# Attention in tiles of 128 tokens of one row, and the first expert's weights brought in one part in three tiles

## The chip, the cores and the metric

The kernel runs on one core of a Trainium2 chip. The metric is the time that the device takes for one launch, in microseconds (us): before, the median of three runs was 1137.16 us (1136.15 to 1142.16). The chip's engines are named as in the profile: PE is the matrix engine (TensorE) and PEld its weight loads, DVE the VectorE, ACT the ScalarE, POOL the GpSimd, SP the SyncE, which here only issues transfers; a name with a q behind it (SPq) is an engine's queue of transfers.

## The reference, cut to what matters

```python
def _attn_ref(q, k, v):                 # each 8 rows x 8 heads x 576 tokens x 64
    scores = scale * np.matmul(q, k.transpose(0, 1, 3, 2))
    gamma = 1.0 - 2.0 ** (-5.0 - np.arange(H, dtype=np.float32))
    rel = pos[:, None] - pos[None, :]
    Dmat = np.where(rel >= 0, gamma[:, None, None] ** rel[None, :, :], 0.0)
    return np.matmul(scores * Dmat[None, :, :, :], v)

def reference(...):
    attn_out = _attn_ref(q, k, v)
    x = attn_out.transpose(0, 2, 1, 3).reshape(B * S, H * D)   # 4608 tokens x 512
    x = _moe_ref(x, w_gate, w1, w2)          # 8 experts; every token goes to its best one
    return _moe2_ref(x, w_gate, w1, w2)      # 8 experts; each takes 576 tokens
```

The attention has no softmax: it is causal, with a decay of gamma to the power of the distance. So it can be computed a piece of a row at a time, with a state of 64x64 per head that is carried from piece to piece: outputs of a piece = (its queries times the state before it) + (masked scores inside the piece, times its values).

## The kernel before, in words

The program runs setup, then `attention`, then the two expert layers. Attention gives 36 tiles of 128 tokens x 512 channels (the rows of X), computes the gate's logits of the first expert layer for each, and stores the tiles to memory (`Xs`). The expert layers start when attention is over; the first expert's rows are gathered and turned while attention still runs its last tiles.

A tile before is 64 tokens of each of two batch rows: `pr, j = divmod(t, 9)`, row pair `pr` and position `j` of nine. Tokens of the one row lie in partitions 0 to 63, those of the other in 64 to 127. `wk` and `ld` are pools of buffers in on-chip memory, `ps` one of accumulators.

Attention's stages are listed in `stages`, each with an offset: in step `s` of the loop at the end of `attention`, stage `f` with offset `off` works on tile `s - off`. Every instruction of that loop keeps its written place on its engine. One step does, in this order on PE:

- `scores`: the products of keys and queries (`pS<-qT,kT`), the queries times the state (`pO<-st,qT`, left out for j = 0), the update of the state (`pS<-vf,k`, left out for j = 8). Each is 16 matmuls of 64x64x64 in fp32, four at a time in the four quadrants of the array (`ZW`). DVE then masks the scores (`s`) and adds the update to the state (`st`).
- `xlow`, of the tile two steps ago: one f16 matmul that leaves the low part of the turned output (`less`), then eight small f16 matmuls for the logits (`tp<-wg1s,xTh`). ACT makes the low part `xTl`.
- `kturn`, of the tile two steps ahead: four transposes of k (`tp<-ct,k`), copied out by ACT.
- `logits`: four small matmuls with `xTl`.
- `outputs`: 16 matmuls of masked scores and values (`pO<-vf,s`, `pO<-vs,s`); DVE then writes the rows `xr`. The values `vf` are scaled on POOL, which also copies half of them to the other partitions (`vs`).
- `xturn` of the tile one step ago, `qturn` of the tile two steps ahead: four transposes each.
- `route`, once for a group of up to four tiles (`starts`): the choice of the expert and its weight, on DVE, ACT and POOL.

`load` brings k, q and v of the tile six steps ahead, as two transfers each (a half of the partitions each), issued by SP in the same written order, in which `store` also stands.

`early` is a generator of which the loop takes one part per step from step `AFTER` = 24 on. Its first part issues the first three pieces of the first expert's first weights (`stage<-in_moe_w_dram`, 512 KB each); from two steps later on, each of four parts casts a piece to f16 (`w1h` on ACT, the low part on DVE or POOL); then come the lists and the gather of the 384 rows that the first expert takes from the first 27 tiles, and their normalising and turning.

In the profile all instructions of the loop have the line L102, that of the helper which keeps the order, so tiles are told apart by their names.

Of the kernel before, what the change touches and what calls it, by code (L numbers as in the profile page):

```python
# [21 lines left out]
BIG = 1048576.0  # L22
TA = 27
SA = 3
AFTER = 24
LEAD_IN = 6
T0 = (76, 88)
LATE = 3
SOON = 3
# [14 lines left out]
def consts_np():  # L44
    import numpy as np
    p=np.arange(128)
    g=1.0-2.0**(-5.0-np.arange(8))
    cols=[]
    for j in range(9): cols.append(g[None,:]**(63-p%64-64*j)[:,None])
    for j in range(9): cols.append(g[None,:]**(p%64-63.0+64*j)[:,None]*2.0**-3)  # L50
    tok=np.zeros((128,36))
    for t in range(36):
        pr,j=divmod(t,9)
        tok[:,t]=(2*pr+p//64)*576+64*j+p%64
    cols.append(tok)
    cols.append(np.eye(128))
    j=p[:,None]; i=p[None,:]
    cols.append((i[:,:64]>=j%64)*1.0)
# [5 lines left out]
CO=dict(gk=(0,72),go=(72,144),tok=(144,180),id=(180,308),m=(308,372),lt=(372,500),p=(500,501),blk=(501,509),sel=(509,525))  # L64

class K: pass

# [48 lines left out]
def attention(k, q, kk_, v, wg1, X, after):  # L116
    tc = k.tc
    nc = InOrder(tc, k.nc)
# [9 lines left out]
    D = [K() for _ in range(NT)]  # L128
    for t, d in enumerate(D):
        d.t = t  # L130
        d.pr, d.j = divmod(t, 9)
# [8 lines left out]
    half = lambda n: slice(64 * n, 64 * n + 64)  # L140
    at = lambda n, d: k.c(n)[:, 8 * d.j:8 * d.j + 8]
    zh = lambda x: x.rearrange("p (h z) d -> p z h d", z=2)

    def load(d):
# [15 lines left out]
    ZW = ((0, 0), (1, 1), (0, 1), (1, 0))  # L160

    def across(pt, x, more=False):

# [13 lines left out]
    def qturn(d):  # L177
        d.qT = turned(d, d.iq, "qT")

    state = [None]  # L180
    pend = []

    def scores(d):
# [3 lines left out]
        pS = ps.tile([128, 2, 512], F32, name="pS")  # L187
        s = pS[:, :, 0:256].rearrange("p z (h i) -> p z h i", i=64)
        n = pS[:, :, 256:512].rearrange("p w (h e) -> p w h e", e=64)
# [3 lines left out]
        for hp in range(4 if d.j else 0):  # L193
            for z, w in ZW:
                mm(d.o[half(w), z, hp, :], d.qT[half(z), hp, half(w)], state[0][half(z), w, hp, :], start=hp == 0, stop=False)
        if d.j < 8:
            for hp in range(4):
                for w, z in ZW:
                    h = 2 * hp + z
                    mm(n[half(z), w, hp, :], d.ik[half(w), h, :], d.vf[half(w), h, :], start=True, stop=True)  # L200
        d.s = wk.tile([128, 2, 4, 64], F32, name="s", bufs=2)
        nc.vector.tensor_tensor(d.s, s, k.c('m')[:, None, None, :].to_broadcast([128, 2, 4, 64]), op=OP.mult)
        if d.j < 8:
            t = wk.tile([128, 2, 4, 64], F32, name="st", bufs=3)
            if d.j:
                nc.vector.tensor_tensor(t, n, state[0], op=OP.add)
            else:
                nc.vector.tensor_copy(t, n)
            state[0] = t

    def outputs(d):
        for hp in range(4):
            for z, w in ((0, 0), (0, 1), (1, 0), (1, 1)):
                r = w ^ z
                mm(d.o[half(w), z, hp, :], d.s[half(r), z, hp, :], d.vs[half(r), hp, :] if z else d.vf[half(r), 2 * hp, :],
                   start=hp == 0 and d.j == 0, stop=hp == 3)
        p = P[d.g]
        if d.gj == 0:
            p.lgs = wk.tile([128, 9, 8], F32, name="lgs")
# [11 lines left out]
    def xlow(d):  # L231
        d.xl = wk.tile([128, 4, 128], F16, name="xTl", bufs=3)
        f = lambda x: x.rearrange("p c i -> p (c i)")
        mm(f(d.pt), k.less8, f(d.xh), start=False, stop=True)
        nc.scalar.activation(d.xl, d.pt, AF.Copy, scale=256.0)
        d.lg = ps.tile([128, 8], F32, name="tp", bufs=4)
        for c in range(4):
            for n in range(2):
                mm(d.lg, d.xh[:, c, :], wg1[:, c, 8 * n:8 * n + 8], start=c + n == 0, stop=False)

    def logits(d):
        for c in range(4):
            mm(d.lg, d.xl[:, c, :], wg1[:, c, 0:8], start=False, stop=c == 3)
        nc.scalar.activation(P[d.g].lgs[:, d.gj, :], d.lg, AF.Copy)

    def route(d):
        p = P[d.g]
        if d.gj < p.n - 1:
            return
        N = p.n  # L250
        T = slice(p.t0, p.t0 + N)
        L = p.lgs[:, :N, :]
# [12 lines left out]
        es = wk.tile([128, 9], F32, name="es")[:, :N]  # L265
        nc.vector.tensor_reduce(es, ex, op=OP.add, axis=AX.X)
        nc.vector.tensor_scalar(es, es, 1e-9, None, op0=OP.add)
        gt = wk.tile([128, 9], F32, name="gt")[:, :N]
        nc.vector.reciprocal(gt, es)
        nc.gpsimd.tensor_copy(p.xrows[:, :N, 513], k.c('tok')[:, T])  # L270
        nc.gpsimd.tensor_copy(p.xrows[:, :N, 512], gt)
        pend.append(p)
# [15 lines left out]
    store()  # L288
    for _ in after:
        pass  # L290
    k.nc = nc.nc
    ctx.close()

# [32 lines left out]
    k.wn = k.xn = 0  # L326


def load_half(k, o, w, n, dve=0, spare=False, steps=True, behind=False):


    tc, nc = k.tc, k.nc
# [23 lines left out]
    stages = []  # L356
    for i in range(3):
        load(i)
    for i in range(4):
        yield  # L360
        t = stages[i]
# [275 lines left out]
    nc.vector.tensor_copy(k.cnt, pb[:, 1, :])  # L637


def early(k, X, w1):  # L640


    nc = k.nc
    first = load_half(k, k.w[0], w1, 1, 2)
    next(first)
    yield
    yield
    for _ in range(4):
        next(first, None)
        yield  # L650
# [936 lines left out]
def program(tc, q, kk, v, wg1, w11, w12, wg2, w21, w22, consts, out, dbg=None):  # L1587
# [10 lines left out]
    k.wgl = split_gate(k, wg2, "wg2")  # L1598
    select_setup(k)
    k.w = {0: K()}  # L1600
    attention(k, q, kk, v, g1, X, early(k, X, w11[0]))
    open_ffn(k)
    rest = moe1(k, X, X1, w11, w12)
    k.pin = False
# [35 lines left out]
```

## Time and profile before

| | us |
|---|---|
| median of three runs | 1137.16 (1136.15 to 1142.16) |
| the profiled execution, its own time | 1137.33 |
| its span in the trace | 1135.3 |
| PE busy over the span | 1034.0 |
| DVE busy | 595.7 |
| ACT busy | 433.9 |
| POOL busy | 295.8 |

The span is what the trace covers; 2.0 us of the execution lie outside it. Busy times are sums over the whole span, so they don't say which engine sets the pace in attention, which is the first fifth of it: there, the rows by stage and by wait further down have to be read. A duration in the trace runs from an instruction's start to its end; matmuls overlap, so what a group of them takes on PE is the distance between the starts of two groups.

### The profile page before, as it was taken

How to read it: one execution, taken by the hardware profiler on the slowest of the kernel's cores; microseconds unless marked ns; L12 is line 12 of the kernel's file. 1: busy time of each engine (PE TensorE's matmuls, PEld its weight loads, DVE VectorE, ACT ScalarE, POOL GpSimd, SP SyncE). 2: the span in 40 equal slices, each digit the busy share in tenths (PEclk: the TensorE clock that was granted, in tenths of full speed). 3: DMA queues.
4: the chain of work that ended last, by engine and by line, in shares of the span. 5: the costliest groups of instructions: out<-in, count | busy, mean ns of one | idle time of the engine just before them, and what ended most of it. 6: DMA issues, size and time to landing. Idle time of an engine off the chain costs nothing. (4 is left out here: it accounts for less than half of the span.)

```text
span 1135.3 us, 28053 instructions
## 1 busy us (share of the span) xinstructions
PE 1034.0 (91%) x11515; PEld 666.8 (59%) x11515; DVE 595.7 (52%) x1589; ACT 433.9 (38%) x747; POOL 295.8 (26%) x569
## 2 busy tenths in 40 slices
PE   5888958688999999999979989998999999899996
PEld 4777746555656564747447534655465756567572
DVE  2334425568566665648553366847565656634140
ACT  2444434447354554546442133423232333234240
POOL 4342333313213021212140022333133141341101
PEclk9998988979999999999989999999999999999998
DMA  7787889449777777878786033377475673774221
GB/s 167 160 212 183 191 223 217 135 130 256 187 158 195 163 195 171 179 178 209 204 172 110 11 108 124 122 182 162 113 172 119 160 176 104 199 200 139 85 71 43
DMA packets 308663, 178.41 MB, mean 157 GB/s; under 512 B 242544, under 2 KB 275312, under 8 KB 308528
## 3 DMA queue, kind: packets, MB, share of 16 engines
q1 hardware_dynamic: 298064, 144.20, 53.2%
q0 software_dynamic: 10464, 32.34, 9.1%
q8 instruction: 93, 1.52, 0.6%
q14 instruction: 42, 0.34, 0.1%
HBM read 116.78 MB, written 31.28 MB: 130 GB/s over the span
## 5 line engine op out<-in xcount | busy, mean ns | idle before, releaser
L487 PE MATMUL ph<-xT,w1h 128*128 128x320 f16 (+4 forms) x2048 | 367.4, 296 | 6.3 <-DVE hl L493 3.2
L487 PEld LDWEIGHTS <-w1h 128*128 128x128 f16 x2048 | 197.3, 99 | 77.4 <-issue 13.1
L487 PE MATMUL ph<-xT,w1l 128*128 128x320 f16 (+4 forms) x1024 | 230.9, 296 | 0.0
L513 PE MATMUL py<-w2h,hh 128*128 128x512 f16 x536 | 204.1, 381 | 2.2 <-DVE key L1268 2.2
L513 PE MATMUL py<-w2h,hl 128*128 128x512 f16 x536 | 203.9, 380 | 0.0
L513 PE MATMUL py<-w2l,hh 128*128 128x512 f16 x536 | 203.9, 380 | 0.0
L513 PEld LDWEIGHTS <-hh 128*128 128x128 f16 x1072 | 103.2, 98 | 119.0 <-issue 3.6
L492 ACT ACTIVATE hh<-ph 128x576 f16<-128x576 f32 (+4 forms) x136 | 83.5, 614 | 194.1 <-PE ph L487 189.9
L493 DVE SCALAR_TENSOR_TENSOR hl<-ph,hh 128x576 f16<-128x576 f32 (+4 forms) x136 | 97.2, 715 | 76.8 <-ACT hh L492 75.6
L487 PEld LDWEIGHTS <-w1l 128*128 128x128 f16 x1024 | 99.9, 99 | 32.7 <-issue 0.7
L373 DVE SCALAR_TENSOR_TENSOR w1l<-stage,w1h 128x1024 f16<-128x1024 f32 x60 | 73.1, 1223 | 60.1 <-ACT w1h L370 59.4
L513 PEld LDWEIGHTS <-hl 128*128 128x128 f16 x536 | 52.5, 98 | 60.4 <-issue 0.8
L373 DVE SCALAR_TENSOR_TENSOR w2l<-stage,w2h 128x1024 f16<-128x1024 f32 x64 | 78.1, 1222 | 6.0 <-ACT w2h L370 4.6
L418 ACT ACTIVATE x1r<-py 128x512 bf16<-128x512 f32 x40 | 23.9, 597 | 119.2 <-PE py L513 78.9
L370 ACT ACTIVATE w2h<-stage 128x1024 f16<-128x1024 f32 x64 | 66.9, 1047 | 0.0
L370 ACT ACTIVATE w1h<-stage 128x1024 f16<-128x1024 f32 x60 | 62.2, 1047 | 4.4 <-DMA stage<-in_moe_w_dram 4.4
L404 POOL DMA_INDIRECT xg<-X1s,ix x40 | 45.6, 1139 | 50.8 <-DVE zf L1372 31.2
L102 DVE TENSOR_TENSOR s<-pS,ct 128x512 f32<-128x512 f32 x36 | 24.8, 688 | 64.4 <-PE pS L102 64.4
L102 POOL TENSOR_TENSOR vf<-v,ct 128x512 f32<-128x512 f32 x36 | 37.5, 1042 | 74.8 <-DMA v<-in_v_dram 64.0
L1446 POOL DMA_INDIRECT out_dram<-x1r,ti x20 | 22.2, 1110 | 130.0 <-ACT x1r L1445 106.8
L571 POOL COPY x1r<-sc 128x1 f32<-128x1 f32 x37 | 12.1, 328 | 156.1 <-DMA X1s<-x1r 84.5
L1446 POOL DMA_INDIRECT out_dram<-w2T,ti x20 | 21.4, 1071 | 109.8 <-ACT w2T L1445 85.3
(358 smaller groups left out, 1479.3 us busy)
## 6 DMA issues: line engine op xcount, KB each, us to landing
stage<-in_moe_w_dram SPq DMA_DIRECT2D x128, 512.0 KB, 4.4
k<-in_k_dram SPq DMA_DIRECT2D x72, 128.0 KB, 4.1
q<-in_q_dram SPq DMA_DIRECT2D x72, 128.0 KB, 4.3
v<-in_v_dram SPq DMA_DIRECT2D x72, 128.0 KB, 4.0
X1s<-x1r SPq DMA_DIRECT2D x33, 257.0 KB, 3.7
Xs<-xr SPq DMA_DIRECT2D x6, 1028.0 KB, 6.2
Xs<-xr SPq DMA_DIRECT2D x3, 771.0 KB, 6.1
xg<-X1s,ix POOLq DMA_INDIRECT x40, 4.3
```

The source lines that it names most:

```text
L102: return lambda *args, **kw: self.tc.keep_in_program_order(f(*args, **kw))
L370: d = nc.scalar.activation(at(h, i), t, AF.Copy, scale=128.0)
L373: d = nc.vector.scalar_tensor_tensor(at(l, i), t, 128.0, at(h, i), op0=OP.mult, op1=OP.subtract)
L404: nc.gpsimd.indirect_dma_start(out=xg[:M], out_offset=None, in_=src, in_offset=bass.IndirectOffsetOnAxis(ap=gidx[:M], axis=0))
L418: d = nc.scalar.activation(q.bitcast(mybir.dt.bfloat16), x, AF.Square, accum_out=sc[:, 0:1])
L487: pe(k, nc.tensor.matmul(ph[:, z, :b], x[:, c, F], xT[:, y + c, a:a + b], start=i == 0, stop=i == 11))
L492: nc.scalar.activation(oh, src, AF.Relu)
L493: nc.vector.scalar_tensor_tensor(ol, src, 0.0, oh, op0=OP.max, op1=OP.subtract)
L513: pe(k, nc.tensor.matmul(py, x[:, f, S], y[:, f, :], start=i == 0, stop=i == 23))
L571: nc.gpsimd.tensor_copy(xr[:, 513:514], sc[:, 5:6])
L1446: nc.gpsimd.indirect_dma_start(out=out2 if tail else out, out_offset=bass.IndirectOffsetOnAxis(ap=ti, axis=0), in_=y, in_offset=None)
```

## The change

A tile becomes 128 tokens of one row. Of a row's 576 tokens four such tiles are made, which leaves 64; the leftovers of two rows make a tile as before (`tail`). In a row pair the tiles alternate between the two rows: n = 0 to 7 is piece n//2 of row n%2, n = 8 the tail. So there are 32 tiles of 128 tokens of one row (eight of them the first of their row) and 4 tails. The same 128 x 36 tokens are in the 27 tiles and in the 9 after them, in another order. The state is kept per row.

On PE a tile that is not a tail now has: `begun` 8 matmuls of 64 columns for the queries times the state, each with 64 of the array's rows; `scores` 8 of 128 columns, each with 64 rows, then the state's update as 8 of 64 columns, now in a `tp` buffer; `outputs` 8 of 64 columns that use the whole array. All of it stays fp32. The logits' first matmuls are 4 of 16 columns in place of 8 of 8 columns, and stand in `logits`; `kturn` stands behind it. On DVE the masked scores are 128x1024 in place of 128x512, the state's update 128x256 in place of 128x512, and `route` has one more addition. The copies `vs` on POOL are gone. `load` issues one transfer of 128 partitions for each of k, q and v.

The first expert's weights leave `early`: they get a generator of their own, which takes a part at step 4 and then at every third step (`CAST`), with the first three pieces' loads in three parts (`spread`) and all low parts on POOL. What is left of `early` starts at step 30, where it stood before.

```diff
-AFTER = 24
+CAST = (4, 3)
+EARLY = (30, 1)
...
     def load(d):
         for src, name in ((kk_, "k"), (q, "q"), (v, "v")):
             t = ld.tile([128, 8, 64], F32, name=name, bufs=dict(k=7, q=5, v=5)[name])
-            for w in range(2):
-                nc.sync.dma_start(t[half(w)], src[2 * d.pr + w, :, half(d.j), :].rearrange("h p d -> p h d"))
+            if d.tail:
+                for w in range(2):
+                    nc.sync.dma_start(t[half(w)], src[d.b + w, :, 512:576, :].rearrange("h p d -> p h d"))
+            else:
+                nc.sync.dma_start(t, src[d.b, :, 128 * d.j:128 * d.j + 128, :].rearrange("h p d -> p h d"))
...
-        d.vs = wk.tile([128, 4, 64], F32, name="vs", bufs=3)
-        for w in range(2):
-            nc.gpsimd.tensor_copy(d.vs[half(1 - w)], zh(d.vf)[half(w), 1])
...
+    def begun(d):
+
         d.pO = ps.tile([128, 2, 512], F32, name="pO")
         d.o = d.pO[:, :, 0:256].rearrange("p z (h d) -> p z h d", d=64)
...
+                for z in range(2):
+                    mm(d.o[:, z, hp, :], d.qT[half(z), hp, :], state[d.b][half(z), hp, :], start=hp == 0, stop=False)
+
+    def scores(d):
+
+        pS = ps.tile([128, 2, 4, 128], F32, name="pS")
+        d.s = wk.tile([128, 2, 4, 128], F32, name="s", bufs=2)
...
         for hp in range(4):
-            for z, w in ZW:
-                mm(s[half(w ^ z), z, hp, :], d.kT[half(z), hp, half(w)], d.qT[half(z), hp, half(w)], start=True, stop=True)
...
+            for z in range(2):
+                mm(pS[:, z, hp, :], d.kT[half(z), hp, :], d.qT[half(z), hp, :], start=True, stop=True)
+        n = ps.tile([128, 4, 64], F32, name="tp", bufs=4)
+        for hp in range(4):
+            for z in range(2):
+                mm(n[half(z), hp, :], d.ik[:, 2 * hp + z, :], d.vf[:, 2 * hp + z, :], start=True, stop=True)
+        nc.vector.tensor_tensor(d.s, pS, k.c('m')[:, None, None, :].to_broadcast([128, 2, 4, 128]), op=OP.mult)
+        t = wk.tile([128, 4, 64], F32, name="st", bufs=5)
...
+                else:
+                    mm(d.o[:, z, hp, :], d.s[:, z, hp, :], d.vf[:, 2 * hp + z, :], start=hp == 0 and d.j == 0, stop=hp == 3)
...
-    stages = [(scores, 0), (xlow, 2), (kturn, -2), (logits, 2), (outputs, 0), (xturn, 1), (qturn, -2), (route, 2)]
+    stages = [(begun, 0), (xlow, 2), (scores, 0), (logits, 2), (kturn, -2), (outputs, 0), (xturn, 1), (qturn, -2), (route, 2)]
...
-        if s >= AFTER:
-            next(after, None)
+        for g, at0, step in after:
+            if s >= at0 and (s - at0) % step == 0:
+                next(g, None)
```

How the instructions stand: first PE, from the end of one step into the next. Before, with 16 matmuls in each row of scores, state and update:

```order
L102 MATMUL tp<-ct,xr 128x128 x4
L102 MATMUL tp<-ct,q 128x128 x4
L102 MATMUL pS<-qT,kT 64x64 x16
L102 MATMUL pO<-st,qT 64x64 x16
L102 MATMUL pS<-vf,k 64x64 x16
L102 LDWEIGHTS less_64
L102 MATMUL tp<-xTh,less_64 128x512
```

The same place on PE after the change (all lines of the loop are L105 there):

```order
L105 MATMUL tp<-ct,k 128x128 x4
L105 MATMUL pO<-vf,s 128x64 x8
L105 MATMUL tp<-ct,xr 128x128 x4
L105 MATMUL tp<-ct,q 128x128 x4
L105 MATMUL pO<-st,qT 128x64 x8
L105 LDWEIGHTS less_64
L105 MATMUL tp<-xTh,less_64 128x512
L105 MATMUL pS<-qT,kT 128x128 x8
L105 MATMUL tp<-vf,k 64x64 x8
```

Half as many matmuls of attention stand in a step, `less` now lies between the queries times the state and the scores, and the outputs' matmuls have 128 columns of weights where they had 64.

Then SP's queue, at the step in which the first expert's weights are first asked for. Before, at step 24:

```order
L102 DMA v<-in_v_dram 64x8x64 x2
L102 DMA stage<-in_moe_w_dram 128x4x256 x3
L102 DMA k<-in_k_dram 64x8x64 x2
L102 DMA q<-in_q_dram 64x8x64 x2
L102 DMA v<-in_v_dram 64x8x64 x2
L102 DMA Xs<-xr 128x4x514
```

After, at step 4:

```order
L105 DMA v<-in_v_dram 128x8x64
L105 DMA stage<-in_moe_w_dram 128x4x256
L105 DMA k<-in_k_dram 128x8x64
L105 DMA q<-in_q_dram 128x8x64
L105 DMA v<-in_v_dram 128x8x64
L105 DMA Xs<-xr 128x4x514
```

One piece stands in the queue where three stood together; the second and the third piece stand three and six steps further on.

Last ACT, where the first piece is cast. Before, at step 26:

```order
L102 ACTIVATE xTh<-tp 128x512
L102 ACTIVATE qT<-tp 128x512
L102 ACTIVATE w1h<-stage 128x4x256
L102 ACTIVATE xTl<-tp 128x512
L102 ACTIVATE kT<-tp 128x512
L102 ACTIVATE lgs<-tp 128x8
```

After, at step 13:

```order
L105 ACTIVATE xTh<-tp 128x512
L105 ACTIVATE qT<-tp 128x512
L105 ACTIVATE ex<-lg 128x32
L105 ACTIVATE w1h<-stage 128x4x256
L105 ACTIVATE xTl<-tp 128x512
L105 ACTIVATE lgs<-tp 128x16
L105 ACTIVATE kT<-tp 128x512
```

The cast `w1h` stands ahead of the same tile's `xTl` in both; it came two steps behind the first piece's load in SP's queue, and now comes nine steps behind it.

## Rows read from the trace of the kernel before

**Rows 1.** Windows: stretch, length, busy of PE PEld DVE ACT POOL, PEclk, DMA share, GB/s

```profile
13.19:235.69 222.50, 173.84 (x5245) 144.65 (x5245) 94.11 (x232) 93.32 (x200) 77.99 (x136) 0.92 0.77 185
235.69:1135.30 899.61, 855.87 (x6255) 519.30 (x6254) 499.67 (x1340) 337.48 (x543) 210.82 (x392) 0.98 0.59 150
```

**Rows 2.** What PE's idle time in attention ended with: us, times

```profile
  issue: 21.1, 24
  ACT xTl L102: 15.0, 5
  DVE s L102: 5.8, 3
  DMA k<-in_k_dram: 1.9, 2
```

**Rows 3.** Two windows from issue gap to issue gap on PE, columns as in Rows 1

```profile
30.46:35.21 4.75, 4.42 (x128) 3.60 (x128) 1.98 (x3) 2.35 (x5) 1.83 (x3) 1.00 0.77 171
35.21:39.97 4.76, 4.33 (x127) 3.55 (x127) 1.98 (x3) 2.30 (x5) 1.83 (x3) 1.00 0.78 172
```

**Rows 4.** DMA queues from 20 to 150 us: packets, MB, share of 16 engines

```profile
q8 instruction: 28, 0.46, 1.5%
```

**Rows 5.** DVE's timeline, output rows of tiles 0, 24 and 35

```profile
21.52 0.69 DVE L102 TENSOR_TENSOR xr<-pO,ct 128x512 f32<-128x512 f32 x1 [1.13 <-PE pO L102]
...
151.25 0.69 DVE L102 TENSOR_TENSOR xr<-pO,ct 128x512 f32<-128x512 f32 x1 [1.83 <-PE pO L102]
...
229.01 0.69 DVE L102 TENSOR_TENSOR xr<-pO,ct 128x512 f32<-128x512 f32 x1 [1.25 <-PE pO L102]
```

**Rows 6.** PE's timeline, one step without a gap: start us, us, records

```profile
115.74 0.70 PE L102 MATMUL pS<-qT,kT 64*64 64x64 f32 x32
116.25 0.65 PE L102 MATMUL pO<-st,qT 64*64 64x64 f32 x32
116.72 0.65 PE L102 MATMUL pS<-vf,k 64*64 64x64 f32 x32
117.30 0.39 PE L102 MATMUL tp<-xTh,less 128*128 128x512 f16 x1
117.53 0.34 PE L102 MATMUL tp<-wg1s,xTh 128*128 128x8 f16 x8
117.73 0.64 PE L102 MATMUL tp<-ct,k 128*128 128x128 f32 x4
...
118.56 0.27 PE L102 MATMUL pO<-vf,s 64*64 64x64 f32 x2
...
119.19 0.65 PE L102 MATMUL tp<-ct,xr 128*128 128x128 f32 x4
119.68 0.60 PE L102 MATMUL tp<-ct,q 128*128 128x128 f32 x4
120.21 0.69 PE L102 MATMUL pS<-qT,kT 64*64 64x64 f32 x32
```

**Rows 7.** One of the page's costliest groups: busy us, mean ns | idle before

```profile
L373 DVE SCALAR_TENSOR_TENSOR w1l<-stage,w1h 128x1024 f16<-128x1024 f32 x60 | 73.1, 1223 | 60.1 <-ACT w1h L370 59.4
```

**Rows 8.** Timelines of ACT, PE and SP's queue around the first expert's weights

```profile
162.97 1.72 SPq L102 DMA_DIRECT2D stage<-in_moe_w_dram  x3
...
168.46 1.06 ACT L102 ACTIVATE w1h<-stage 128x1024 f16<-128x1024 f32 x1 [10.82 <-DMA stage<-in_moe_w_dram]
...
170.06 0.27 PE L102 MATMUL tp<-wg1s,xTl 128*128 128x8 f16 x4 [10.91 <-ACT xTl L102]
```

**Rows 9.** Windows, tile 26's turned rows to tile 27's, columns as in Rows 1

```profile
155.99:172.69 16.70, 4.68 (x122) 3.86 (x123) 3.12 (x5) 3.18 (x6) 4.70 (x7) 0.71 0.93 217
```

**Rows 10.** PE's timeline where the first expert's rows are listed

```profile
191.75 0.18 PE L102 MATMUL tp<-incA,lt_h 128*128 128x1 f16 x1 [0.60 <-DVE incA L102]
...
193.78 1.13 PE L102 MATMUL pS<-qT,kT 64*64 64x64 f32 x32
```

**Rows 11.** SP's queue, a tile's loads of q and v, both halves

```profile
160.28 1.27 SPq L102 DMA_DIRECT2D q<-in_q_dram  x2
161.65 1.27 SPq L102 DMA_DIRECT2D v<-in_v_dram  x2
```

More of the change, by code (lines that the diff above doesn't have):

```diff
@@ L47, in consts_np @@
     g=1.0-2.0**(-5.0-np.arange(8))
+    at=[128*j+p for j in range(4)]+[512+p%64]
     cols=[]
-    for j in range(9): cols.append(g[None,:]**(63-p%64-64*j)[:,None])
-    for j in range(9): cols.append(g[None,:]**(p%64-63.0+64*j)[:,None]*2.0**-3)
+    for x in at: cols.append(g[None,:]**(127.0-x)[:,None])
+    for x in at: cols.append(g[None,:]**(x-127.0)[:,None]*2.0**-3)
     tok=np.zeros((128,36))
     for t in range(36):
-        pr,j=divmod(t,9)
-        tok[:,t]=(2*pr+p//64)*576+64*j+p%64
+        pr,n=divmod(t,9)
+        tok[:,t]=(2*pr+(p//64 if n==8 else n%2))*576+at[n//2]
     cols.append(tok)
@@ L57, in consts_np @@
     j=p[:,None]; i=p[None,:]
+    cols.append((i>=j)*1.0)
     cols.append((i[:,:64]>=j%64)*1.0)
@@ L63, in consts_np @@
     return np.ascontiguousarray(np.concatenate(cols,1).astype(np.float32))
-CO=dict(gk=(0,72),go=(72,144),tok=(144,180),id=(180,308),m=(308,372),lt=(372,500),p=(500,501),blk=(501,509),sel=(509,525))
+CO=dict(gk=(0,40),go=(40,80),tok=(80,116),id=(116,244),m=(244,372),m64=(372,436),lt=(436,564),p=(564,565),blk=(565,573),sel=(573,589))
 class K: pass
@@ L130, in attention @@
         d.t = t
-        d.pr, d.j = divmod(t, 9)
+        pr, n = divmod(t, 9)
+        d.j, d.b = n // 2, 2 * pr + n % 2
+        d.tail = n == 8
     starts = [0, 4, 8, 12, 16, 20, 24, 27, 30, 33, 35, 36]
@@ L142, in attention @@
     zh = lambda x: x.rearrange("p (h z) d -> p z h d", z=2)
+    ZW = ((0, 0), (1, 1), (0, 1), (1, 0))
     def load(d):
@@ L154, in pre @@
         nc.gpsimd.tensor_tensor(d.vf, d.iv, at('gk', d)[:, :, None].to_broadcast([128, 8, 64]), op=OP.mult)
-        d.vs = wk.tile([128, 4, 64], F32, name="vs", bufs=3)
-        for w in range(2):
-            nc.gpsimd.tensor_copy(d.vs[half(1 - w)], zh(d.vf)[half(w), 1])
     mm = partial(nc.tensor.matmul, skip_group_check=True)
-    ZW = ((0, 0), (1, 1), (0, 1), (1, 0))
     def across(pt, x, more=False):
@@ L178, in qturn @@
         d.qT = turned(d, d.iq, "qT")
-    state = [None]
+    state = {}
     pend = []
-    def scores(d):
+    def begun(d):
         d.pO = ps.tile([128, 2, 512], F32, name="pO")
         d.o = d.pO[:, :, 0:256].rearrange("p z (h d) -> p z h d", d=64)
-        pS = ps.tile([128, 2, 512], F32, name="pS")
-        s = pS[:, :, 0:256].rearrange("p z (h i) -> p z h i", i=64)
-        n = pS[:, :, 256:512].rearrange("p w (h e) -> p w h e", e=64)
-        for hp in range(4):
-            for z, w in ZW:
-                mm(s[half(w ^ z), z, hp, :], d.kT[half(z), hp, half(w)], d.qT[half(z), hp, half(w)], start=True, stop=True)
[L193 to L209, printed above, removed]
@@ new lines, in begun @@
+        for hp in range(4 if d.j else 0):
+            if d.tail:
+                for z, w in ZW:
+                    mm(d.o[half(w), z, hp, :], d.qT[half(z), hp, half(w)], state[d.b + w][half(z), hp, :], start=hp == 0, stop=False)
+            else:
[4 more added lines that the diff above has]
+        d.s = wk.tile([128, 2, 4, 128], F32, name="s", bufs=2)
+        if d.tail:
+            for hp in range(4):
+                for z, w in ZW:
+                    mm(pS[half(w), z, hp, 0:64], d.kT[half(z), hp, half(w)], d.qT[half(z), hp, half(w)], start=True, stop=True)
+            nc.vector.tensor_tensor(d.s[:, :, :, 0:64], pS[:, :, :, 0:64],
+                                    k.c('m64')[:, None, None, :].to_broadcast([128, 2, 4, 64]), op=OP.mult)
+            return
+        for hp in range(4):
+            for z in range(2):
+                mm(pS[:, z, hp, :], d.kT[half(z), hp, :], d.qT[half(z), hp, :], start=True, stop=True)
+        n = ps.tile([128, 4, 64], F32, name="tp", bufs=4)
+        for hp in range(4):
+            for z in range(2):
+                mm(n[half(z), hp, :], d.ik[:, 2 * hp + z, :], d.vf[:, 2 * hp + z, :], start=True, stop=True)
+        nc.vector.tensor_tensor(d.s, pS, k.c('m')[:, None, None, :].to_broadcast([128, 2, 4, 128]), op=OP.mult)
+        t = wk.tile([128, 4, 64], F32, name="st", bufs=5)
+        if d.j:
+            nc.vector.tensor_tensor(t, n, state[d.b], op=OP.add)
+        else:
+            nc.vector.tensor_copy(t, n)
+        state[d.b] = t
@@ L211, in outputs @@
     def outputs(d):
         for hp in range(4):
[L213 to L216, printed above, removed]
+            for z in range(2):
+                if d.tail:
+                    for w in range(2):
+                        mm(d.o[half(w), z ^ w, hp, :], d.s[half(w), z ^ w, hp, 0:64], d.vf[half(w), 2 * hp + (z ^ w), :],
+                           start=False, stop=hp == 3)
+                else:
+                    mm(d.o[:, z, hp, :], d.s[:, z, hp, :], d.vf[:, 2 * hp + z, :], start=hp == 0 and d.j == 0, stop=hp == 3)
@@ L217, in outputs @@
         p = P[d.g]
         if d.gj == 0:
-            p.lgs = wk.tile([128, 9, 8], F32, name="lgs")
+            p.lgs = wk.tile([128, 4, 16], F32, name="lgs")
             p.xrows = xp.tile([128, 4, W], F32, name="xr")
@@ L235, in xlow, with logits @@
         nc.scalar.activation(d.xl, d.pt, AF.Copy, scale=256.0)
-        d.lg = ps.tile([128, 8], F32, name="tp", bufs=4)
+    def logits(d):
+        lg = ps.tile([128, 16], F32, name="tp", bufs=4)
         for c in range(4):
-            for n in range(2):
-                mm(d.lg, d.xh[:, c, :], wg1[:, c, 8 * n:8 * n + 8], start=c + n == 0, stop=False)
-    def logits(d):
+            mm(lg, d.xh[:, c, :], wg1[:, c, 0:16], start=c == 0, stop=False)
         for c in range(4):
-            mm(d.lg, d.xl[:, c, :], wg1[:, c, 0:8], start=False, stop=c == 3)
-        nc.scalar.activation(P[d.g].lgs[:, d.gj, :], d.lg, AF.Copy)
+            mm(lg[:, 0:8], d.xl[:, c, :], wg1[:, c, 0:8], start=False, stop=c == 3)
+        nc.scalar.activation(P[d.g].lgs[:, d.gj, :], lg, AF.Copy)
     def route(d):
@@ L251, in route @@
         T = slice(p.t0, p.t0 + N)
-        L = p.lgs[:, :N, :]
+        L = wk.tile([128, 4, 8], F32, name="lg")[:, :N, :]
+        nc.vector.tensor_tensor(L, p.lgs[:, :N, 0:8], p.lgs[:, :N, 8:16], op=OP.add)
         mx = wk.tile([128, 9], F32, name="mx")[:, :N]
@@ L285, in attention @@
                 f(D[s - off])
-        if s >= AFTER:
-            next(after, None)
+        for g, at0, step in after:
+            if s >= at0 and (s - at0) % step == 0:
+                next(g, None)
     store()
-    for _ in after:
-        pass
+    for g, _, _ in after:
+        run(g)
     k.nc = nc.nc
@@ L326, in moe_setup, with load_half @@
     k.wn = k.xn = 0
-def load_half(k, o, w, n, dve=0, spare=False, steps=True, behind=False):
+def load_half(k, o, w, n, dve=0, spare=False, steps=True, behind=False, spread=False):
     tc, nc = k.tc, k.nc
@@ L358, in load_half @@
         load(i)
+        if spread and i < 2:
+            yield
     for i in range(4):
@@ L637, in moe1_tables, with early @@
     nc.vector.tensor_copy(k.cnt, pb[:, 1, :])
-def early(k, X, w1):
+def early(k, X):
     nc = k.nc
[L644 to L650, printed above, removed]
     k.nA = k.cp.tile([128, 4], F32, name="nA")
@@ L1600, in program @@
     k.w = {0: K()}
-    attention(k, q, kk, v, g1, X, early(k, X, w11[0]))
+    attention(k, q, kk, v, g1, X, [(load_half(k, k.w[0], w11[0], 1, spread=True), *CAST), (early(k, X), *EARLY)])
     open_ffn(k)
```

## The prediction

> **What bounds the kernel now.** I read the windows first. Attention takes from 13.19 to 235.69 us, 222.5 us, and what follows 899.6 [rows 1]. The code behind attention is the same and its lists hold the same tokens, so I hold the 899.6 fixed and ask when attention ends. No engine is full in attention: PE is busy 173.8 of 222.5 us, DVE 94, ACT 93, POOL 78, the DMA engines 0.77 [rows 1].
>
> Next comes what PE waited for. Its largest item is "issue", 21.1 us in 24 gaps, in which nothing that the profile shows was missing [rows 2]. Between two such gaps lie 127 or 128 matmuls and as many weight loads each time, 256 instructions in 4.75 us [rows 3] (a record or so is missing). The queue that carries instructions moves 28 packets in 130 us, one in 4.64 us [rows 4]. I read this as PE's instructions arriving in blocks of 256, no faster than one block in 4.75 us. Count a step: an fp32 matmul is two matmul records and two loads, a transpose or f16 matmul one and one. A full tile has 64 fp32 matmuls, 12 transposes, `less` and 12 logits' matmuls: 256 + 24 + 2 + 24 = 306. The tiles j = 0 and j = 8 lack 16 matmuls: 242. The mean over nine is (7 x 306 + 2 x 242) / 9 = 292, and 292/256 x 4.75 = 5.42 us per step. Measured from tile 0's output rows to tile 24's: (151.25 - 21.52) / 24 = 5.41 [rows 5]. A step without a gap takes 120.21 - 115.74 = 4.47 [rows 6]. So the number of PE's instructions sets the pace, not the work in them.
>
> The second item is one wait of 10.91 us on `xTl`: ACT stands 10.82 us at the cast of the first expert's first piece, which SP asked for only at 162.97 behind its other transfers [rows 8]. From tile 26's turned rows to tile 27's pass 16.70 us in place of 4.47: 12.2 lost [rows 9]. [...]
>
> **The change part by part.** Instructions first: a full tile has 24 fp32 matmuls in place of 64 in scores, state, update and outputs (8 + 8 + 8 and 8 more for the outputs make 32), thus 128 records, and 24 for transposes, 2 for `less`, 16 for logits: 170. At 256 per 4.75 us that is 3.15 us, which is under the step's work (below), so the gaps should go.
>
> The work on PE goes up, because four quadrants no longer share every matmul. From the step without a gap [rows 6]: a block of 16 quadrant matmuls takes 116.72 - 116.25 = 0.47, in four rounds of two passes of 64 columns, 0.058 a pass. The first block after the turns takes 0.51, 0.04 more; behind the last block the change to the whole array adds 117.30 - 116.72 - 0.47 = 0.11. So a switch costs 0.15. Four transposes take 119.68 - 119.19 = 0.49, of which 0.05 is the first one's load: 0.11 a pass of 128 columns. `less` takes 0.23, eight logits' matmuls 0.20. After the change a full tile has, in order:
>
> - queries times state, 8 matmuls x 2 passes of 64 columns, the two row halves side by side: 8 x 0.058 = 0.47
> - `less` 0.23
> - scores, 8 x 2 passes of 128 columns, halves side by side: 8 x 0.11 = 0.88
> - update, 8 x 2 passes of 64 columns, two column halves side by side: 0.47
> - logits 0.20
> - turns of k, xr and q: 3 x 0.44 = 1.32
> - outputs, 8 x 2 passes of 64 columns in the whole array: 16 x 0.058 = 0.93
> - five switches (before the state, `less`, scores, update and logits): 0.75
>
> That is 5.25, and with 0.05 for waits 5.3. A row's first tile lacks the state's part and two switches: 4.5, taken as 4.6. A tail (quadrants as before, no update) is at 4.2. The sum is 24 x 5.3 + 8 x 4.6 + 4 x 4.2 = 180.8 us. Before, by the same counting, 28 x 4.47 + 8 x 3.85 = 156.0: the change adds 24.8 us of work to PE.
>
> Two of these values no row shows. **The outputs** load 128 columns of weights for every 64 that they move. Lower end: the load hides behind the move, 0.058 a pass. Upper end: load and move follow each other like a pass of 128, 0.11 a pass, +0.83 a tile, x32 = +26.6. The nearest row is the turns' first load, which costs 0.05 where nothing hides it [rows 6], under the 0.058 of the move; I take 0.058. [...]
> **The halves side by side**: before they are always in quadrants. If the two row halves of the state's part took turns, +0.47 x 24 = +11; for the scores +0.88 x 32 = +28, both +39. The quadrants of before run four at a time, so I take side by side.
>
> DVE: the masked scores grow from 512 to 1024 elements; the row of 128x1024 is 1.22 [rows 7]. From the end of the scores PE has update, switches, logits and k's turns, 0.47 + 0.20 + 0.44 + 0.30 = 1.4, before the outputs need it: 1.22 and the way to and from PE are just hidden. If PE's cover were gone it would cost 0.1 to 0.2 a tile, +5. The next tile's `begun` needs the outputs' accumulator, which DVE's `xr` (0.69 [rows 5]) sets free; PE turns xr of the tile before and q meanwhile (0.88), as it did. POOL loses `vs` (0.85) and gains the low part of four pieces; its values are due two steps ahead. `route`'s addition is small work on DVE. All at nothing.
>
> SP: three transfers in place of six a tile, with the same bytes. A pair of halves took 1.27 [rows 11], so three of these are 3.8 us a tile; one of 128 partitions costs between half of that and all of it. Both are below 5.3.
>
> The first expert's weights: the load comes nine steps ahead of its cast (47 us) where it was two, and the queue holds one piece at a time. ACT's cast of 1.06 us [rows 8] lies in a step in which ACT has 2.4 of 5.3 us. [...]
>
> The sum, in two ways. From the end: first scores at 13.2, steps 180.8, the start-up that tile 0 shows (21.52 - 13.19 = 8.3 to its output rows, where a step gives 3.6 by then [rows 5, 6]): 4.7; route's delays at eight groups, by the four other `xTl` waits (15.0 - 10.9 = 4.1) [rows 2]: 3.2; the list of the first expert's rows, 193.78 less 191.05 (the last turns' end), 2.7, and 2.0 for the blocks behind it, of which the scores take 1.13 in place of 0.70 [rows 6, 10]; waits on DVE in the normalising steps 4.7 of the 5.8 [rows 2]; from tile 35's output rows to the end 235.69 - 229.01 = 6.7 [rows 1, 5], of which 0.5 is in the step. 13.2 + 180.8 + 4.7 + 3.2 + 4.7 + 4.7 + 6.2 = 217.5, or 18.2 earlier than 235.69. By difference: +24.8 work, -14.0 stall, and the gaps' cost: (5.41 - 4.33) x 24 = 25.9 in the first 24 steps (4.33 the mean of the counted work) and some 3 in the rest: -28.9; together -18.1. The profiled execution took 1137.33 (span 1135.3, 2.0 outside it), within 0.02% of the median, so about 1119; I add 1 for waits that a longer step brings: **1120 us**.
>
> **The rivals.** A change within 0.5% (5.7 us: 1131.5 to 1142.8) can't be told from none.
>
> 1. *The transfers pace the stage.* The DMA engines are at 0.77 [rows 1] and SP issues without a pause. Then the step stays at 5.41 and only the stall goes: 1137.3 - 14.0 + 1 = 1124. Against it: PE waited for k only 1.9 us [rows 2].
> 2. *The state's row halves take turns*: +11, 1131.
> 3. *Other side: the outputs' loads aren't hidden.* With 0.11 a pass 1120 + 26.6 = 1147, with the state's halves taking turns as well 1158. It makes the kernel slower from 17/512 = 0.034 above 0.058 a pass, 0.092. For it: no fp32 weights of 128 columns under 64 moved columns stand in the trace; against it the 0.05 of rows 6.
> 4. *The gaps aren't a matter of counts.* If they stay as they are, 21.1 us, the work's 24.8 is paid: 1137.3 + 24.8 - 14.0 = 1148. Against it: 5.42 counted, 5.41 measured.
> [...]
> 5. *A new wait in each step* on the single accumulators of scores or outputs, or on DVE's masked scores, 0.5 a full tile: 24 x 0.5 + 8 x 0.5 = 16, 1136.
>
> **How the numbers follow.** Chances: the forecast 0.50 (its own range 1111 to 1129: half of the late waits saved below, +9 for DVE's cover and route above); rival 1 0.12; rival 2 0.10; rival 3 0.13; rival 4 0.07; rival 5 0.08. The range reaches from 1111 to 1142, which leaves out rivals 3 and 4, 0.20. Faster: forecast, rival 1 and half of rival 2, 0.67; same: the other half and rival 5, 0.13; slower 0.20.
>
> **What the profile after would show.** PE's "issue" idle in attention close to nothing; steps of 5.3 us; 16 passes of outputs in 0.93 and of scores' eight in 0.88; no ACT wait above 1 us at the first expert's casts; first matmul of the first expert at about 218 us; the rest 899.6. I am wrong if outputs take 1.7 us (rival 3), if gaps of 0.5 us and more stay every 256 instructions though PE needs fewer (rival 4), or if PE waits for k, q or v in most steps (rival 1).

## The result

The change made the kernel slower: 1155.23 us median of four runs (1153.53 to 1157.17), beside 1139.66 for four runs of the kernel before (1136.15 to 1142.18); the ratio is 1.0139, 95% interval 1.0101 to 1.0178. The forecast was 1120, the range 1111 to 1142.

The windows of the profile after (span 1155.3, own time 1157.17): attention, the rest, and one full step. The columns are those of [rows 1].

```profile
12.23:252.71 240.48, 228.28 (x3054) 196.91 (x3054) 100.86 (x240) 95.99 (x200) 55.06 (x70) 0.97 0.78 170
252.71:1155.30 902.59, 859.88 (x6255) 520.92 (x6254) 499.50 (x1341) 337.91 (x543) 206.53 (x392) 0.97 0.60 150
106.46:113.12 6.66, 6.66 (x87) 5.84 (x86) 2.25 (x3) 2.47 (x6) 2.17 (x3) 1.00 0.99 281
```

Attention ends at 252.71 where it ended at 235.69 [rows 1]: 17.0 of the 20.0 us by which the span grew. The 3.0 us behind it I don't ascribe to the change: in two of the runs below, which differ from it only in attention, that stretch takes 898.5 and 904.3. PE is now busy 228.3 of 240.5 us, with 3054 matmul records in place of 5245. What its idle time in that window ended with:

```profile
its engine sat idle before it (us, times) until:
  DVE s L105: 4.0, 4
  ACT xTh L105: 3.2, 8
  ACT xTl L105: 2.7, 5
  DVE G L105: 1.1, 1
  DVE xr L105: 0.2, 1
```

Beside [rows 2]: "issue" is gone (21.1 before), so is the wait at the first expert's cast (10.9). PE's idle time fell from 48.7 to 12.2 us, about as forecast (28.9 for the gaps and 12.2 for the stall), and its busy time grew by 54. PE's timeline shows where, read as in [rows 6]:

```profile
106.46 1.11 PE L105 MATMUL pO<-st,qT 64*128 64x64 f32 x16
107.50 0.39 PE L105 MATMUL tp<-xTh,less 128*128 128x512 f16 x1
107.82 1.16 PE L105 MATMUL pS<-qT,kT 64*128 64x128 f32 x16
108.91 0.69 PE L105 MATMUL tp<-vf,k 128*64 128x64 f32 x16
109.53 0.26 PE L105 MATMUL tp<-wg1s,xTh 128*128 128x16 f16 x4
109.64 0.24 PE L105 MATMUL tp<-wg1s,xTl 128*128 128x8 f16 x4
109.74 0.64 PE L105 MATMUL tp<-ct,k 128*128 128x128 f32 x4
110.31 2.00 PE L105 MATMUL pO<-vf,s 128*128 128x64 f32 x16
112.14 0.61 PE L105 MATMUL tp<-ct,xr 128*128 128x128 f32 x4
112.59 0.60 PE L105 MATMUL tp<-ct,q 128*128 128x128 f32 x4
113.12 1.11 PE L105 MATMUL pO<-st,qT 64*128 64x64 f32 x16
```

From start to start, the outputs take 112.14 - 110.31 = 1.83 us where 0.93 was forecast, the state's part 1.04 where 0.47 and a switch were. Those two are the groups whose weights have 128 columns and whose move has 64. The scores (128 columns of both) take 1.09 and the update (64 of both) 0.62, as forecast to within a tenth.

### The profile page after: what moved, and what is told of

Read it like the earlier page. It is cut to its first block, busy times and chain, and to the rows that moved or that the text cites. A ratio compares the mean times of both kernels' runs of the same rounds, so it can differ in the third digit from the quotient of the medians.

```text
span 1155.3 us, 23540 instructions
## 1 busy us (share of the span) xinstructions
PE 1092.3 (95%) x9323; PEld 720.7 (62%) x9323; DVE 602.4 (52%) x1598; ACT 437.0 (38%) x747; POOL 267.7 (23%) x501
## 5 line engine op out<-in xcount | busy, mean ns | idle before, releaser
L534 PEld LDWEIGHTS <-hl 128*128 128x128 f16 x536 | 52.5, 98 | 60.2 <-issue 0.6
L105 DVE TENSOR_TENSOR s<-pS,ct 128x1024 f32<-128x1024 f32 (+1 forms) x36 | 41.8, 1162 | 66.5 <-PE pS L105 66.5
L105 PE MATMUL pO<-vf,s 128*128 128x64 f32 (+1 forms) x640 | 68.7, 267 | 4.5 <-DVE s L105 4.0
L105 PEld LDWEIGHTS pO<-vf,s 128*128 128x128 f32 (+1 forms) x640 | 64.0, 181 | 10.6 <-DVE s L105 8.8
L105 DVE TENSOR_TENSOR xr<-pO,ct 128x512 f32<-128x512 f32 x36 | 24.9, 692 | 63.2 <-PE pO L105 54.2
```

The lines of the kernel that those rows point to most:

```text
L105: return lambda *args, **kw: self.tc.keep_in_program_order(f(*args, **kw))
L534: pe(k, nc.tensor.matmul(py, x[:, f, S], y[:, f, :], start=i == 0, stop=i == 23))
```

## The experiments

**Which property of the matmuls costs the time.** Theory A: an fp32 load of 128 columns takes about 0.115 us (an estimate from the 1.83 above, over 16 passes), twice one of 64, and a pass takes the longer of load and move. Theory B: such a load takes 0.058, and stands in series with the move or, in the state's part, the two row halves take turns.

First, both groups with weights of 64 columns again:

```diff
-                for z in range(2):
-                    mm(d.o[:, z, hp, :], d.qT[half(z), hp, :], state[d.b][half(z), hp, :], ...)
+                for z, w in ZW:
+                    mm(d.o[half(w), z, hp, :], d.qT[half(z), hp, half(w)], state[d.b][half(z), hp, :], ...)
...
-                    mm(d.o[:, z, hp, :], d.s[:, z, hp, :], d.vf[:, 2 * hp + z, :], ...)
+                    for w in range(2):
+                        mm(d.o[half(w), z, hp, :], d.s[:, z, hp, half(w)], d.vf[:, 2 * hp + z, :], ...)
```

> The changed kernel with the weights of the queries times the state and of the outputs in pieces of 64 columns again (quadrants for the first, two column halves with all 128 rows for the second); everything else as changed. Theory A (an fp32 load of 128 columns takes some 0.115 us, twice one of 64 columns, and a pass takes the longer of its load and its move): outputs fall from 1.84 to 0.93 us a tile, the state's part from 1.04 to some 0.5, the full step from 6.66 to 5.2 or 5.3, and the time to 1113 to 1121. Theory B (a load of 128 columns takes 0.058 and stands in series with the move, or takes turns with that of the other row half): outputs fall only to 16 x 0.087 = 1.39, time about 1127. Both: no issue gaps at 234 instructions a step of 5.2 us.

Measured: 1120.57 us, ratio to the kernel before 0.9862 (0.9830 to 0.9894). Windows of attention and of one full step, and PE's timeline in it:

```profile
12.00:219.70 207.70, 195.73 (x3948) 161.60 (x3945) 101.58 (x239) 95.24 (x200) 54.82 (x70) 0.98 0.88 197
219.70:1118.20 898.50, 856.40 (x6255) 519.91 (x6254) 499.51 (x1341) 337.76 (x543) 205.72 (x392) 0.98 0.60 150
125.64:131.18 5.54, 5.54 (x119) 4.66 (x118) 2.43 (x5) 2.46 (x6) 1.71 (x3) 1.00 0.88 192
```

The timeline:

```profile
125.64 0.69 PE L105 MATMUL pO<-st,qT 64*64 64x64 f32 x32
126.27 0.39 PE L105 MATMUL tp<-xTh,less 128*128 128x512 f16 x1
...
129.07 1.15 PE L105 MATMUL pO<-vf,s 128*64 128x64 f32 x32
130.16 0.66 PE L105 MATMUL tp<-ct,xr 128*128 128x128 f32 x4
```

The state's part falls from 1.04 to 0.63, the outputs from 1.83 to 1.09, of which I put some 0.15 (an estimate: 1.09 less 16 x 0.058) to the change of the array's shape that these column halves need. The step falls by 1.12 us with 64 instructions more in it, and attention ends 33.0 us earlier (219.7). The time is that of theory A; the full step is 5.54 where A said 5.2 or 5.3. No issue gaps come back.

Then the move alone, doubled, with the weights as the change has them (the second copy of the values goes to unused columns):

```diff
-                    mm(d.o[:, z, hp, :], d.s[:, z, hp, :], d.vf[:, 2 * hp + z, :], ...)
+                    mm(d.pO[:, z, 128 * hp:128 * hp + 128].rearrange("p (a d) -> p a d", a=2), d.s[:, z, hp, :],
+                       d.vf[:, 2 * hp + z:2 * hp + z + 1, :].to_broadcast([128, 2, 64]), ...)
```

> The changed kernel with each output matmul moving 128 columns in place of 64 (the same 64 values twice, the second copy goes to unused columns of the accumulator). Weights are the same 128 columns. Theory A: the load of 0.115 already sets the pass, a move of 128 columns takes 0.11, so the outputs stay at 1.84 us a tile and the time at 1155, plus or minus 3. Theory B (load and move in series): a pass takes 0.058 + 0.109, the outputs 2.67 a tile, the time 1155 + 27 = 1182.

Measured: 1158.91 us, one run. PE's timeline, the outputs:

```profile
103.96 2.05 PE L105 MATMUL pO<-vf,s 128*128 128x128 f32 x16
105.85 0.60 PE L105 MATMUL tp<-ct,xr 128*128 128x128 f32 x4
```

Twice the columns moved take 1.89 in place of 1.83, 0.118 a pass in place of 0.114. Record by record, the weight loads of the outputs start 0.112 us apart in the profile of the change. So the move of 64 columns is hidden behind something of that length that goes with the weights; B in series, which wants 2.67, is out. B's other form, turns, is out by the records of the state's part in the profile of the change: the loads of the two row halves start 0.007 us apart, and the next pair 0.112 later.

And the state's part alone in quadrants (the first half of the first diff):

> The changed kernel with only the queries times the state back in quadrants of 64 columns, outputs as changed. Theory A, and B as well: from 1.04 to some 0.5 us a full tile, 24 x 0.55 = 13 less: 1142. Rival C (these matmuls are slow for what they move or where they write, not for their weights): 1.04 stays, 1155.

Measured: 1146.57 us, one run: 10.6 us less than the profiled run of the change (1157.17), 8.7 less than its median. PE's timeline:

```profile
102.34 0.69 PE L105 MATMUL pO<-st,qT 64*64 64x64 f32 x32
102.97 0.39 PE L105 MATMUL tp<-xTh,less 128*128 128x512 f16 x1
```

0.63 again (some 0.5 was expected: the switch behind it stays), 0.41 x 24 = 9.8 us: rival C, by which these matmuls are slow for what they move or where they write, is out. The rest of the 34.7 us (1155.23 less 1120.57), some 25, is the outputs.

**What the spreading of the first expert's weights is worth.** The kernel before with the change's schedule for these weights alone:

```diff
-AFTER = 24
+CAST = (4, 3)
+EARLY = (30, 1)
...
```

> The kernel before with only the first expert's weights brought in one part in three steps from step 4 on (all low parts on POOL). If the wait of 10.9 us and the slow clock behind it were the whole price of the weights: 12 to 14 less, about 1124, and steps stay at 5.4 with issue gaps of 21 us in all. Rival: the transfers only collide elsewhere, with the loads of q, k and v or with the instructions' arrival, and half of it is given back: about 1131.

Measured: 1137.60 us (10 runs), ratio 1.0019 (0.9998 to 1.0040): nothing is won, and both expectations miss. What PE's idle time ended with from 13.19 to 235:

```profile
  issue: 25.4, 20
  DMA k<-in_k_dram: 8.4, 5
  DVE s L103: 4.8, 2
  ACT xTl L103: 3.3, 3
```

The wait on `xTl` falls by 11.7 against [rows 2], as it should. It comes back as 4.3 us more of "issue" and 6.5 more of k, and the 24 steps of [rows 5] take 141.8 us where they took 129.7: the transfers of the weights now lie among the others there. That they delay these is my reading of the longer waits.

Conversely, the new tiles with the weights brought late:

```diff
-CAST = (4, 3)
+CAST = (24, 1)
...
-[(load_half(k, k.w[0], w11[0], 1, spread=True), *CAST)
+[(late(load_half(k, k.w[0], w11[0], 1, 2)), *CAST)
```

> The kernel of the run with both weights in pieces of 64 columns (1120.6), with the first expert's weights brought as in the kernel before: three pieces asked for together at step 24, casts from step 26. If the spreading carries the gain of these tiles: ACT waits some 10 us at the first cast again and the time is 1130 to 1134. If spreading is worth as little here as it was in the kernel before (1.0019): 1120 plus or minus 3.

Measured: 1125.26 us, ratio 0.9903 (0.9885 to 0.9921); attention ends at 223.6 in place of 219.7. Between both expectations: no wait of 10 us comes back, and the spreading is worth some 4 us here. SP is no longer behind when it asks for the pieces: it asks at 145.56, as the rows of tile 24 are written (145.91), and the first cast, at 157.85, waits for nothing. In the kernel before it asked 17.9 us behind that tile's rows (162.97 against 145.05).

**What bounds the kernel before.** Fewer instructions on PE, by leaving out the queries times the state:

```diff
-        for hp in range(4 if d.j else 0):
+        for hp in range(0):
...
```

> The kernel before without the queries times the state (its 16 matmuls, 64 instructions, of every tile but a row's first, are left out, so the outputs lack that part). If the number of PE's instructions sets the pace (256 in 4.75 us): the mean step has 235 in place of 292 and takes 4.36 in place of 5.41 us, from tile 0's output rows to tile 24's 105 in place of 130 us, with issue gaps every 256 instructions still there. If the gaps are not a matter of counts: each step loses only its work, 0.42 on the mean, so 120 us from tile 0 to tile 24.

Measured: 1136.83 us, one run; attention ends at 235.0, where it ended at 235.7. Both expectations miss. PE's waits from 13.19 to 235, and DVE's timeline, the rows that stand in the place of those in [rows 5]:

```profile
  DMA k<-in_k_dram: 24.7, 11
  ACT xTl L102: 17.9, 9
  DVE s L102: 4.5, 4
  DMA q<-in_q_dram: 4.1, 6
...
  issue: 1.1, 3
```
```profile
21.73 0.69 DVE L102 TENSOR_TENSOR xr<-pO,ct 128x512 f32<-128x512 f32 x1 [2.13 <-PE pO L102]
...
149.58 0.69 DVE L102 TENSOR_TENSOR xr<-pO,ct 128x512 f32<-128x512 f32 x1 [0.60 <-PE pO L102]
```

"issue" is gone with the instructions, 21.1 to 1.1, and the wait for k takes its place, 1.9 to 24.7: the step is 127.85/24 = 5.33 us, from 5.41. So a second limit stands behind the first, the loads: 16 matmuls fewer in most tiles gave back 1.9 us in 24 steps.

Then without the loads of v (q stands in), and without both:

```diff
-        for src, name in ((kk_, "k"), (q, "q"), (v, "v")):
+        for src, name in ((kk_, "k"), (q, "q")):
...
+        d.iv = d.iq
```

> The kernel before without the loads of v (a third of the loads' transfers; q stands in for v, so the outputs are others); all work on the engines as before. Theory D (two limits of about the same pace bound the stage, PE's instructions at 292 a step and the loads of k, q and v, and each hides the other): the step stays at 5.3 to 5.4 us with issue gaps of 21 to 28 us in all, the wait for k goes, and the time falls by the shorter stall at the first expert's weights at most: 1128 to 1137. Theory E (only the loads bound it, and the issue gaps are a mark of PE running out of loaded tiles): steps near 4.5, time about 1105 to 1110.

> Both cuts at once: no queries times the state and no loads of v. Alone, the first changed the time by nothing (1136.8). Theory D: with 235 instructions a step and a third fewer transfers the step falls to 4.4 us or a little under, 105 us from tile 0's output rows to tile 24's where the kernel before takes 130, and the time to 1105 to 1115. If neither instructions nor loads are the limit: 125 us or more, and 1130 or more.

Only attention is compared, since the outputs have other values: the work behind attention can differ with them (the first of these takes 2054.29 us in all, the second 1086.54). Without v:

```profile
  issue: 13.4, 15
  ACT xTl L102: 3.4, 5
```
```profile
20.09 0.69 DVE L102 TENSOR_TENSOR xr<-pO,ct 128x512 f32<-128x512 f32 x1 [0.22 <-PE pO L102]
...
137.36 0.69 DVE L102 TENSOR_TENSOR xr<-pO,ct 128x512 f32<-128x512 f32 x1 [1.83 <-PE pO L102]
```

Without both:

```profile
19.19 0.69 DVE L102 TENSOR_TENSOR xr<-pO,ct 128x512 f32<-128x512 f32 x1 [1.19 <-PE pO L102]
...
120.44 0.69 DVE L102 TENSOR_TENSOR xr<-pO,ct 128x512 f32<-128x512 f32 x1 [0.62 <-PE pO L102]
```

The steps are 4.89 and 4.22 us. Neither limit stands alone (theory E wanted 4.5 without v), and they aren't independent as theory D had it (5.3 without v; its 4.4 or a little under without both is met): with fewer loads the "issue" gaps shrink too, to the 13.4 above from 21.1 in [rows 2]. With both cut, attention ends at 185.6 us, and PE is busy 96.9 of the 101.3 us that these 24 steps take.

**Whether the form of the loads matters.** The run with both weights halved, with each load in two transfers of 64 partitions:

```diff
-                nc.sync.dma_start(t, src[d.b, :, 128 * d.j:128 * d.j + 128, :].rearrange("h p d -> p h d"))
+                for w in range(2):
+                    nc.sync.dma_start(t[half(w)], src[d.b, :, 128 * d.j + 64 * w:128 * d.j + 64 * w + 64, :].rearrange("h p d -> p h d"))
```

> The run with both weights in pieces of 64 columns (1120.6), with k, q and v loaded as two transfers of 64 partitions each, as before; the same bytes. In the kernel before, the loads held a step at 5.3 us when instructions no longer did. If that pace belongs to the 64-partition form: with the weights of the first expert among the loads PE waits for k again (10 to 30 us) and the time is 1130 to 1145. If it belongs to the bytes alone: PE waits for k only at the start, 1119 to 1123.

Measured: 1131.26 us (10 runs), ratio 0.9960 (0.9938 to 0.9982), 10.7 more than with whole loads. PE waits for k again:

```profile
139.91 0.94 PE L105 MATMUL tp<-ct,k 128*128 128x128 f32 x4 [3.38 <-DMA k<-in_k_dram]
```

Windows from 20 to 150 us of the kernel before, of the run with whole loads, and of this one (last two columns: DMA share, GB/s):

```profile
20.00:150.00 130.00, 113.74 (x3562) 94.74 (x3562) 54.20 (x116) 58.22 (x126) 45.72 (x82) 0.97 0.79 188
```
```profile
20.00:150.00 130.00, 127.81 (x2650) 106.51 (x2648) 59.71 (x119) 62.72 (x128) 38.90 (x43) 1.00 1.01 226
```
```profile
20.00:150.00 130.00, 123.53 (x2530) 102.99 (x2534) 59.52 (x117) 59.43 (x122) 37.96 (x41) 0.99 0.86 196
```

Whole loads move 226 GB/s in that stretch and halves 196. (The 188 before are without weights of the first expert, which both others bring in there.) With whole loads SP runs ahead and stands 52.5 of the 130 us waiting for free buffers, with halves 19.1. So the form matters, but less by PE's waits than expected: from 13 to 235 us they are 4.2 in two for k, where 10 to 30 were forecast. Attention ends at 232.3, 12.6 later: 1.5 is lost before the first tile's rows, 5 at the stall shown, and the rest mostly behind 150 us, which I did not take apart.

**Versions beyond.** Three orders and forms on top of both halved weights; each ratio is to the kernel before as it ran beside them. Scores and update directly behind the state's part:

```diff
-    stages = [(begun, 0), (xlow, 2), (scores, 0), (logits, 2), (kturn, -2), (outputs, 0), ...]
+    stages = [(begun, 0), (scores, 0), (xlow, 2), (kturn, -2), (logits, 2), (outputs, 0), ...]
```

> The run with both weights in pieces of 64 columns, with scores and update directly behind the state's part and the low part of the output, k's turns and the logits behind them: two changes of the array's shape fewer a step. By the cost of such a change in the kernel before (0.11 to 0.15 each), 0.2 to 0.3 less than 5.54 us a full step, 6 to 9 less in all: 1112 to 1115. Rival: the logits now wait for ACT's low part (0.6 us behind its matmul, of which k's turns cover 0.57), and nothing is won: 1120.

Measured: 1125.27 us, ratio 0.9908 (0.9891 to 0.9924). The rival, and worse: PE waits for `xTl` 35 times, 9.2 us in all, and a full step takes 5.70. With the logits behind the outputs:

```diff
+    stages = [(begun, 0), (scores, 0), (xlow, 2), (kturn, -2), (outputs, 0), (logits, 2), ...]
```

> The run with both weights in pieces of 64 columns, in this order: state's part, scores and update, the low part of the output, k's turns, outputs, logits, turns. The logits no longer wait for ACT (0.17 us and a start later in each step of the run before), and two changes of the array's shape are gone. If PE still sets the pace: 0.2 us less than 5.54 a full step, 1112 to 1115. Rival: the DMA engines, busy 0.95 to 1.0 of the time in the run with both weights halved, are at their limit: PE now waits for k or q, and the time stays at 1118 to 1121.

Measured: 1119.26 us, ratio 0.9877 (0.9833 to 0.9920): a full step takes 5.42, so half of the 0.2 is there, and the time can't be told from that of both halved weights. The rival's time is met and its reason isn't: from 20 us on PE never waits for k or q. With that order, the scores' weights in pieces of 64 columns too:

```diff
-            for z in range(2):
-                mm(pS[:, z, hp, :], d.kT[half(z), hp, :], d.qT[half(z), hp, :], start=True, stop=True)
+            for z, w in ZW:
+                mm(pS[half(w), z, hp, :], d.kT[half(z), hp, half(w)], d.qT[half(z), hp, :], start=True, stop=True)
```

> The run with the logits late (1119.3), with the scores' weights in pieces of 64 columns too (16 matmuls in quadrants, each moving 128 columns; a step has 266 instructions in place of 234). If PE's work sets the pace: the move of 128 columns (0.11 a pass) already covers the load, and only the change of shape between the state's part and the scores goes, 0.1 to 0.2 a full step: 1113 to 1117. If the arrival of PE's instructions is the limit at 266 in 5.3 us: issue gaps come back and the time stays at 1119 or rises to 1124.

Measured: 1124.32 us, ratio 0.9882 (0.9822 to 0.9943). Its undisturbed step takes 5.22 us, as forecast, but the four runs (1117.99 to 1125.94) show no gain over those of the run before (1117.26 to 1124.82). PE's waits have the instructions again, at 266 a step, and a longer wait on DVE (5.0 us before), which I did not follow up:

```profile
  DVE s L105: 10.4, 6
  issue: 6.0, 7
```

## Why the prediction was wrong

**The change part by part, outputs: this step failed.** The sum took 0.058 us a pass and named 0.11 as the upper end; it is 1.83/16 = 0.114. That is 0.90 x 32 = 29 us, within 3 of the price that rival 3 had (26.6). The row I chose by was the wrong one: the first of four turns costs 0.05 more than the others, and I read that as the whole of its load. The turns' own pace of 0.11 was the better row: it holds a load of 128 columns and a move of 128, and can't tell which of the two sets it. The run with the doubled move tells: 128 columns of weights cost some 0.115 us a pass whether 64 or 128 are moved (1.83 and 1.89 for 16). With 64 columns of both a pass takes 0.058 (0.47 for eight, [rows 6]), half of that, and the 0.05 of the first turn did not bear on it.

**The halves side by side: right in itself, but the term was too small.** The state's part has the same 128 columns of weights. Its 8 pairs of passes at 0.115 make 0.92, and with the switch 1.04, 0.42 more than forecast, 10 us in 24 tiles. The halves do run side by side: their loads start 0.007 us apart. So rival 3 came true, and a price near rival 2's 11 us came with it, but not by its turns: both terms have one cause, the columns of the weights. That rival 3's upper time, 1158, is near the profiled run's 1157 is luck in this part: it holds the 11 of the turns where the state's loads cost 10.

**The start-up term: a misread row.** [Rows 5] are the output rows of tiles 1, 25 and 35, not 0, 24 and 35 (their distance, 24 steps, and 5.41 stand). Two steps fit into the 8.3 us (tile 0's rows are written at 16.96), and the 4.7 us were not there. 217.5 + 29 + 10 - 4.7 = 251.8, where attention ended at 252.7.

**The gaps: gone as forecast, for half of the reason.** They vanish in the changed kernel, so rival 4 is out, and return at 266 instructions in 5.2 us. But the sum booked them as 28.9 us that fewer instructions alone would give back, and the run without the state's part, with 235 a step, shows that they would have given back next to nothing (1.9 us in 24 steps): the loads of the kernel before stand at nearly the same pace. Rival 1 held for the kernel before. In the changed one it doesn't: PE waits for no load in its steps of 6.66 us, and not in those of 5.54 either as long as the loads are whole. "A pair of halves took 1.27" costed SP's issue alone and missed what whole loads are worth (10.7 us).

**The stall of 14.0: not a term of its own.** [Rows 9] show 12.2 of it; the other 1.8 no run shows by itself. What the trace of the kernel before shows in its place is the step behind the stall: 6.37 us where 4.47 were (PE starts the turned rows at 172.50 and at 178.87), with a granted clock of 0.50 from 169 to 176.5 us. Spread over the loads of the kernel before, it comes back in full (1.0019); in the new tiles spreading is worth some 4 us. That the forecast's two sums agreed was no check: both rest on the same count of PE's work (180.8 us), and without the misread 4.7 the first gives 212.8, so that they no longer agree.

**What held:** DVE's masked scores (no wait on `s` in the step shown), POOL, the first expert's casts without a wait, the rest unchanged to 3 us. With the weights' pieces back at 64 columns the kernel takes 1120.6, within 1 us of the forecast, which is in part luck: its full steps are 0.24 longer than the forecast's (some 0.15 of it, by the estimate above, the one more switch that the column halves need), 5.8 us in 24, and the 4.7 of the start-up aren't there.

What stays open: why PE's "issue" gaps are longer with more loads (21.1 us with v, 13.4 without), by the shared DMA engines or by the order in a queue, and what the tiles of before would gain from loads of all 128 partitions at once, which was not tried.

## What to carry to other kernels

In these runs a pass of an fp32 matmul (two to a matmul) took 0.058 us with 64 columns of weights and 64 moved (0.47 for eight), 0.114 with 128 and 64 (1.83 for 16), 0.118 with 128 and 128 (1.89 for 16) and 0.12 with 64 and 128 (0.98 for eight). So cost a pass by the longer of the two; weights of 128 columns under 64 moved ones paid double, and splitting them into column halves or quadrants gave back 34.7 us here. A wait that ends with a resource's arrival is not that resource's price: cut it, and look what stands behind it, before booking it as gain (21.1 us of issue gaps became 24.7 us of waiting for k). Two ways of summing from the same terms are no check of these terms.

## What was unexpected of the hardware

- With k, q and v loaded as one transfer of 128 partitions each, the DMA engines were at 1.01 from 20 to 150 us and moved 226 GB/s; as two of 64 partitions each, 0.86 and 196. The bytes of the whole kernel are the same (1120.6 against 1131.3 us); in that stretch whole loads were further ahead (29.36 MB moved against 25.48).
- PE's issue gaps shrank with the loads: with a third of these gone (v's) they fell from 21.1 us in 24 to 13.4 in 15, with the same instructions on PE.
- Between one shape of sub-arrays and another (64x64 to 64x128) the array paid 0.11 us, as between quadrants and the whole (0.11 in [rows 6]): the scores took 1.10 with `less` between them and the state's part (126.58 to 127.68, both halved weights), 1.09 directly behind it, and 0.98 directly behind it in its own shape (64x64).
